# Spreading a background convolution over four units instead of five, with GpSimd's instructions in smaller pieces

## The chip, the cores and the metric

The kernel runs on one core of one Trainium2 chip. The core has five engines with a queue of instructions each, which start in the order in which the program issued them: TensorE (PE in the profile; PEld is its weight load), VectorE (DVE), ScalarE (ACT), GpSimd (POOL) and SyncE (SP), which here issues the DMAs. The metric is the device time of one execution in microseconds, as the median of several runs.

## The reference

A sequence of 2048 tokens with 1024 channels, in 32-bit floats, passes two kinds of layers in turn, A, B, A, B:

```python
def _A_ref(q, k, v, shift_k, ssm_k, ssm_D):
    ...
    kv = k_shift * v
    ...
    y = y + kv * ssm_D[None, None, :]
    return q * y

def _B_ref(x, w1, b1, w2, b2):
    h = jnp.einsum("bsd,df->bsf", x, w1) + b1
    ...
    h = r * r
    out = jnp.einsum("bsf,fd->bsd", h, w2) + b2
    return out

x = A_q
x = x + _A_ref(_layernorm(x, axis=-1), A_k, A_v, A_shift_k, A_ssm_k, A_ssm_D)
x = x + _B_ref(_layernorm(x, axis=-1), B_w1, B_b1, B_w2, B_b2)
x = x + _A_ref(_layernorm(x, axis=-1), A_k, A_v, A_shift_k, A_ssm_k, A_ssm_D)
x = x + _B_ref(_layernorm(x, axis=-1), B_w1, B_b1, B_w2, B_b2)
```

`k_shift` is a causal convolution of length 4 over `k`; `y` is a causal convolution over the whole sequence, channel by channel, of `kv` with `ssm_k`. It depends on neither `x` nor the layer, so it is computed once. In B, `r` is `h` where positive, and F, the width of `h`, is 3584.

## The kernel before

**The main work.** The tokens are cut into four blocks of 512. One unit is layer B of one block in one of the two rounds; ORDER lists the eight units as pairs (round, block): (0,0), (1,0), (0,1), (0,2), (1,1), (0,3), (1,2), (1,3). Units 5 and 6 are worked together. A unit runs in steps of 12 matmuls of 512 columns (each product is made of three, from a high and a low half of both operands, lines 344 to 346). Kind m1 makes `h`, kind m2 the output. A usual unit has 4 chunks of 28 steps, 112 in all; unit 0 has 134, of which the first 8 belong to the start of the kernel, and unit 1 has 124. 16 steps at the start of unit 0, 28 at its end and 24 at the start of unit 1 work on half a block each, and carry half the tokens. The weights of coming steps are loaded by SP into `wr`, cast by ScalarE into the high half of `whl` (line 1103) and subtracted by VectorE into the low half (line 1111); six `whl` buffers stand in a ring. Some pairs of halves are stored and loaded again later. The m1 result passes ScalarE and VectorE (lines 1588 to 1596) and comes back as the operand of m2; `evict` (line 1711) adds m2's result to the output block. `add_b2` (line 1831) adds the output bias to that block near the start of a unit, on GpSimd, 1024 elements at a time.

**The background work.** The long convolution is computed by blocks of 256 tokens in a transformed space. Token block 0 is done at the start of the kernel. For the others (sb = 1, 2, 3) it runs between the steps of the main loop, as Python generators that issue a few instructions each time they are advanced:

- `fwd_x` and `fwd_g` transform `kv` and `ssm_k`, eight column chunks for each sb, and store the results. Both are advanced once by each `fwd_tick`; FWD_RATE says how many ticks a step of a unit gives them. They share two PSUM banks (`pt`) with the inverse transforms through `take`, `hold` and `give`.
- `prod_stream` goes over sb, 16 groups of channels and three types. For each it loads two operands (`cx`, `cg`, two buffers each), and for the two blocks j = 2 sb and 2 sb + 1 `mult` multiplies them on GpSimd (line 534): 128 x (j + 1) elements on each partition, 384 to 1024, into `cp` (three buffers). Two advances later `red` sums over the blocks on VectorE (line 538). After a group's last product come, each one or more advances later, `fold` and `butterfly` on GpSimd (lines 684, 688, 689), a cast on ScalarE and subtractions on VectorE (lines 563, 570), the inverse transform on TensorE (for sb = 2 and 3 two groups in one), a copy and a store to `yd`.

The result for a token block is needed when the next unit prepares its input. When 18 steps of a unit are left, the main loop calls `close_conv` for the next unit's block, which advances the streams until that block is done. Whatever it issues stands in each engine's queue ahead of the following step.

**The pace.** Each step adds `pace[u]` to `owed`, and `prod_stream` is advanced while something is owed, up to 1.06 times the step's rate; an advance that issued a product returns its size in thousands of elements per partition. In the last 19 steps of a unit the rate is a fifth, in half steps a tenth, and `fwd_tick` isn't called in either. Blocks 1 and 2 share one pace over units 0 to 2, block 3 has its own over units 3 and 4. The pace is the work over the steps, in which the last 19 of a unit count a fifth, less a slack (PACE_SLACK); half steps count in full.

After the convolution is done, and from unit 4 on, `make_t` forms sums of the weights for unit 7 in the buffers that the convolution no longer needs.

Of the kernel before, what the change touches and what calls it, by code (L numbers as in the profile page):

```python
# [19 lines left out]
S, D, F = 2048, 1024, 3584  # L20
P = 128
T = 512
NT = T // P
NB = S // T
# [4 lines left out]
BL = 256  # L29
NBL = S // BL  # L30
BT = T // BL
CG = 64
NG = D // CG
CU = 2 * CG
EPS = 1e-5
ORDER = [(0, 0), (1, 0), (0, 1), (0, 2), (1, 1), (0, 3), (1, 2), (1, 3)]
# [9 lines left out]
AHEAD_0 = 4  # L46
BURST = 1.06
FIN = "GGG"
PACE_SLACK = {1: 74, 3: 10}
PACE_TO = {1: 2}  # L50
PLAIN = 1
FILL = (16, 12, 8)
WINO = (7,)
# [20 lines left out]
PIECES = ((0, 0), (0, 1), (1, 0), (1, 1))  # L74
WLO = {"b": "GGGV", "x": "GGGV"}
PREP_PACE = 0.2
FWD_RATE = {0: 1.4, 1: 1.4, 2: 1.4, 3: 1.1, 4: 1.1, 5: 1}


class Later:  # L80
# [168 lines left out]
def tile_h3_mlp(ctx: ExitStack, tc: tile.TileContext, q, kT, vT, shk, ssmT, ssmD, w1, b1, w2, b2,  # L249
                fwd_t, pro_t, inv_t, sgn_t, out):  # L250
    nc = tc.nc
    V, A, G, PE, SY = nc.vector, nc.scalar, nc.gpsimd, nc.tensor, nc.sync
# [268 lines left out]
    def fwd_tick():  # L521
        for g in streams:
            next(g, None)
# [4 lines left out]
    def prod_stream():  # L528
        lag = plag
        sums, inv = [0, 0], [0, 0]  # L530

        def mult(st, xt, gt, j):
            pr = cv.tile([P, CU, j + 1], F32, name="cp", bufs=3)
            G.tensor_mul(pr.rearrange("p c i -> p i c"), xt[:, 0:j + 1], gt[:, j::-1])  # L534
            st["pr"] = pr

        def red(st, sm, ty, jj):
# [109 lines left out]
        for n, (sb, g, ty) in enumerate(units):  # L647
            while n not in when:
                if (sb, g // 2) in fwd_done:
                    load(n)  # L650
                else:
                    lag.tick()
                    yield None
            while lag.n < when[n] + 2:
                lag.tick()
                yield None
            if ty == 0:
                while sums[0] - sums[1] >= 2:
                    lag.tick()
                    yield None  # L660
                sums[0] += 1
                sm = cv.tile([P, 3, BT, CU], F32, name="sm", bufs=2)
                if g % 2 == 0:
                    pair = {}
            for jj in range(BT):
                j = BT * sb + jj
                st = {"pair": pair}
                mult(st, *got[n], j)
                lag.at(2, red, st, sm, ty, jj)
                if jj == BT - 1:  # L670
                    if ty == 2:
                        lag.at(3, fin, st, sm, sb, g, 0)
                    fill(n)
                lag.tick()
                yield (j + 1) * CU * 1e-3
# [5 lines left out]
        return t[:, e].rearrange("p (n c) -> p n c", c=CG)  # L681

    def fold(E, s):
        E.tensor_add(s[:, 1:3], s[:, 1:3], s[:, 0:1].to_broadcast([P, 2, s.shape[2]]))  # L684

    def butterfly(E, s):
        y = s[:, 1:3].rearrange("p r (j u c) -> p u (r j) c", u=2, c=CG)
# [55 lines left out]
    def prep_a(l, b):  # L743
        mv = pre.tile([P, NT, 2], F32, name="mv", bufs=2)
        xs = [load_x(l, b, 0), load_x(l, b, 1)]
        for _ in range(3):
            yield
        for tt in range(NT):
            stats(xs[tt], mv[:, tt])
            if tt + 2 < NT:  # L750
                xs.append(load_x(l, b, tt + 2))
            yield
            yield
            yield
        ve, sd = rstd_a(mv)
        yield
        lnx[l, b] = mv, rstd_b(ve, sd)
        yield
# [120 lines left out]
    def prep_rows(l, b, kept):  # L879
        yield from prep_a(l, b)  # L880
        mv, r = lnx.pop((l, b))
        for tt in range(NT):
            x = load_x(l, b, tt)
            y = pre.tile([P, D], F32, name="px", bufs=2)
            SY.dma_start(y, YD[b][:, tt])
            for _ in range(4):
                yield
            combine(x, y, mv[:, tt, 0:1], r[:, tt:tt + 1])
            yield
            m = pre.tile([P, 1, 2], F32, name="mv2", bufs=4)  # L890
            stats(x, m[:, 0])
            ve, sd = rstd_a(m)
            yield
            SY.dma_start(X1[b][:, tt], x)
            kept.append(scale_bias(m, ve, sd))
            yield
# [8 lines left out]
    NU = len(ORDER)  # L905
# [671 lines left out]
    pds = prod_stream()  # L1577
# [3 lines left out]
    lag = slag  # L1581
# [246 lines left out]

    def add_b2(st, accs):
        for a in accs:  # L1830
            G.tensor_add(a, a, st["t"])

    def store_out(accs, l, b):
        for tt in range(NT):
# [284 lines left out]
    last_step = {}  # L2119
# [3 lines left out]
    p6_at = {s: i for s, (k, u, c, a, i, *_) in enumerate(steps) if k == "ja" and a == 6}  # L2123
    jb_at = min(s for s, (k, *_) in enumerate(steps) if k == "jb")
    start_step = {u: (last_step[u - 1] + 1 if u else 0) for u in range(NU)}
    work = {sb: 3 * NG * CU * 1e-3 * sum(BT * sb + jj + 1 for jj in range(BT)) for sb in range(1, NB)}
    WIN = {sb: min(u for u in range(NU) if ORDER[u][1] == sb) for sb in range(1, NB)}
    pace = {}
    lo_u = 0
    for sb in range(1, NB):  # L2130
        if WIN[sb] > lo_u:
            group = [x for x in range(sb, NB) if PACE_TO.get(x, x) == PACE_TO.get(sb, sb)]
            hi_u = WIN[group[-1]]
            total = sum(work[x] for x in group)
            n = sum(last_step[u] + 1 - start_step[u] - 19 * (1 - PREP_PACE) for u in range(lo_u, hi_u))
            for u in range(lo_u, hi_u):
                pace[u] = total / (n - PACE_SLACK[sb])
            lo_u = hi_u
    owed = town = 0.0
    fowed = 0.0  # L2140
    accs = []
# [4 lines left out]

    def close_conv(nb):
        while nb not in done:
            if next(pds) is None:
                fwd_tick()  # L2150

    for s, (k, u, c, a, i, tts, w) in enumerate(steps):
        if s < 2 * AHEAD_0:
# [2 lines left out]
        if u != cur_u:  # L2156
            cur_u = u
            if u:
                xT = nxt[0] if u == JU + 2 else nxt
            bst = {}  # L2160
            if u == JU:
                jb = ORDER[JU + 1][1]
                lag.at(10, j_places)
                for tt in range(NT):
                    lag.at(4 + tt, j_rows_load, jb, tt)
                    lag.at(7 + tt, j_rows_norm, rn, tt)
                    lag.at(11 + 3 * tt, j_flip, tt)
                    lag.at(12 + 3 * tt, j_xsums, tt, xT, 0)
                    lag.at(13 + 3 * tt, j_xsums, tt, xT, 1)
            elif u in WINO:  # L2170
                wacc, rp = {}, {}
                lag.at(11, load_wacc, wacc, b)
                lag.at(34, load_b2, bst)
                lag.at(38, add_b2w, bst, wacc)
            else:
                if not (u and direct[u - 1]):
                    accs = []
                    lag.at(5, load_acc, accs, b)
                lag.at(12, load_b2, bst)
                lag.at(16, add_b2, bst, accs)  # L2180
# [17 lines left out]
        if k == "m1":  # L2198
# [9 lines left out]
            for kk in range(4):  # L2208
                t = slice(kk * P, (kk + 1) * P)
# [8 lines left out]
        elif k == "ja":  # L2218
# [9 lines left out]
            for kk in range(4):  # L2228
                t = slice(kk * P, (kk + 1) * P)
# [16 lines left out]
        elif k == "jb":  # L2246
# [9 lines left out]
            for tt in range(NT):  # L2256
                t = slice(tt * P, (tt + 1) * P)
# [7 lines left out]
        elif k == "w2":  # L2265
# [7 lines left out]
            for n in range(2):  # L2273
                t = slice(n * P, (n + 1) * P)
# [11 lines left out]
        else:  # L2286
# [5 lines left out]
            for tt in tts:  # L2292
                t = slice(tt * P, (tt + 1) * P)
# [12 lines left out]
            if direct[u] and c == NCH - 1 and a == 0 and i == 0 and tts[0] == 0:  # L2306
                close_conv(ORDER[u + 1][1])
                spare = []
                closed[0] = True
                while len(spare) + 4 < AHEAD[u]:  # L2310
                    got = take(1, True)
                    if got:
                        spare += got
                    else:
                        fwd_tick()
                        plag.tick()
                closed[0] = False
                nxt = (mw.tile([P, KT, T], F32R, name="xh", bufs=1), mw.tile([P, KT, T], F32R, name="xl", bufs=1))
                ready = set()
                half, evict1, stage = chain(accs, b, *nxt, ready)  # L2320
# [6 lines left out]
        if u == JU:  # L2327
            nxt = []if s == start_step[u] else nxt
        elif u + 1 < NU and not direct[u]:
            n = s - start_step[u]  # L2330
            at = J_PREP if u + 1 == JU else 28
            if n == at:
                pa = prep_a(*ORDER[u + 1])
                if u + 1 == JU:
                    rn = []
                    pa = chain_of(prep_rows(*ORDER[JU + 1], rn), pa)
            elif n > at and pa is not None and next(pa, 0) == 0:
                pa = None
            if u in WINO and left == W_PREP:
                nxt = prep_w(*ORDER[u + 1], lag)  # L2340
            elif u not in WINO and left == 18:
                while pa is not None:
                    if next(pa, 0) == 0:
                        pa = None
                close_conv(ORDER[u + 1][1])
                nxt = prep_b(*ORDER[u + 1], lag)
        if u >= WMAKE and len(done) == NB and not tgen:
            tgen.append(make_t())
# [11 lines left out]
        while todo > 0:  # L2360
            x = next(pds, 0)
# [5 lines left out]
            else:  # L2367
                todo -= x
                owed -= x
        fowed += FWD_RATE.get(u, 2) * (0.0 if busy or len(tts) < NT else 1.0)  # L2370
        while fowed >= 1:
# [52 lines left out]
```

## Time and profile before

| | us |
|---|---|
| median of 3 runs | 2677.67 |
| lowest and highest | 2674.93, 2677.69 |
| the profiled execution | 2678.93 |
| its span in the trace | 2677.1 |

The profile is of one execution. Its page gives each engine's busy time and share, the costliest groups of instructions by line, and the DMA issues; the trace behind it is asked for the waits of an engine, for instructions in order of time, and for tables by stretch of the span. A row of a timeline reads: start, duration, engine, line, operation, what it writes from what it reads, count, and in brackets the idle time of the engine just before with what ended it. A row of waits reads: total us, how often, the longest. The clock is the share of its full speed that TensorE was granted. The row of a line gives the shortest, the median and the longest duration in ns.

### The profile page before, as it was taken

What the parts mean: (1) busy time and instruction counts of PE and PEld (TensorE: products, weight loads), DVE (VectorE), ACT (ScalarE), POOL (GpSimd) and SP (SyncE); (2) the same over time, 40 slices, a digit from 0 to 9 for tenths busy, and PEclk for the clock granted to TensorE, in tenths of its full rate; (3) what the DMA queues carried; (4) which work ended last, traced back from release to release, by engine and by line L of the source; (5) the groups of instructions that cost most, each with busy time, mean ns of one, the idle gap of its engine ahead of it and who ended that gap; (6) DMA issues with size and microseconds to landing.
All of it is one profiled execution on the core that took longest, in us unless ns stands there. A gap on an engine that the chain in (4) does not pass through costs nothing.

```text
span 2677.1 us, 36183 instructions
## 1 busy us (share of the span) xinstructions
PE 2621.7 (98%) x12400; PEld 2195.7 (82%) x12400; DVE 1987.5 (74%) x2993; ACT 1116.0 (42%) x1947; POOL 851.7 (32%) x532
## 2 busy tenths in 40 slices
PE   7999999999999999999999999999999999999999
PEld 7888787888888888888888888887787888788887
DVE  7879888789887877779777777655788674745565
ACT  4454344434444333343333422345655443345443
POOL 2336665355642645427554275100000030001000
PEclk9999999999999999999999999999999999999999
DMA  8789898689989898888987888777899988746556
GB/s 259 260 301 313 294 307 282 240 294 374 339 296 317 315 337 299 267 306 307 337 298 257 308 301 315 266 243 285 304 308 303 367 296 310 265 164 197 174 171 206
DMA packets 390680, 761.59 MB, mean 284 GB/s; under 512 B 45392, under 2 KB 160736, under 8 KB 390496
## 3 DMA queue, kind: packets, MB, share of 16 engines
q1 hardware_dynamic: 390496, 759.28, 82.4%
q8 instruction: 98, 1.61, 0.2%
q14 instruction: 86, 0.70, 0.1%
HBM read 581.92 MB, written 177.21 MB: 284 GB/s over the span
## 4 chain that ended last, share of the span: by engine, by line
PE 76%; DVE 9%; DMA 8%; issue 2%; SPq 2%; ACT 2%; POOL 1%; DVEq 0%; ACTq 0%; POOLq 0%
PE p L344 22%; PE p L345 22%; PE p L346 22%; DMA wr<-w 3%; PE p L1189 2%; PE pt L345 2%; PE pt L344 2%; PE pt L346 2%; DVE whl L1111 1%; DMA whl<-wd_m 1%; DMA cx<-xd 1%; DMA cg<-gd 0%; DVE st L705 0%; SPq L1955 0%; PE pt L429 0%
## 5 line engine op out<-in xcount | busy, mean ns | idle before, releaser
L534 POOL TENSOR_TENSOR cp<-cx,cg 128x384 f32<-128x384 f32 (+5 forms) x288 | 546.1, 1909 | 572.0 <-DVE sm L538 367.0
L344 PE MATMUL p<-xh,whl 128*128 128x512 f32 (+1 forms) x1504 | 576.8, 384 | 4.8 <-ACT fx L1907 2.9
L346 PE MATMUL p<-xh,whl 128*128 128x512 f32 (+1 forms) x1504 | 572.4, 381 | 0.8 <-POOL whl L1111 0.8
L345 PE MATMUL p<-xl,whl 128*128 128x512 f32 (+1 forms) x1504 | 572.4, 381 | 0.1
L1111 DVE TENSOR_TENSOR whl<-wr,whl 128x512 fp32r<-128x512 f32 x535 | 452.2, 858 | 95.6 <-ACT whl L1103 82.6
L1103 ACT CAST whl<-wr 128x512 fp32r<-128x512 f32 x550 | 334.7, 618 | 383.0 <-PE p L346 243.8
L344 PE MATMUL p<-whl,rh 128*128 128x512 f32 x1204 | 475.5, 395 | 3.8 <-ACT whl L1103 2.8
L345 PE MATMUL p<-whl,rh 128*128 128x512 f32 x1204 | 470.7, 391 | 1.3 <-POOL whl L1111 0.8
L346 PE MATMUL p<-whl,rl 128*128 128x512 f32 x1204 | 470.4, 391 | 0.0
L344 PEld LDWEIGHTS p<-xh,whl 128*128 128x128 f32 x1504 | 283.5, 189 | 59.5 <-ACT fx L1907 4.6
L346 PEld LDWEIGHTS p<-xh,whl 128*128 128x128 f32 x1504 | 283.1, 188 | 55.3 <-POOL whl L1111 1.0
L345 PEld LDWEIGHTS p<-xl,whl 128*128 128x128 f32 x1504 | 283.3, 188 | 52.3 <-DVE xl L1502 0.3
L344 PEld LDWEIGHTS p<-whl,rh 128*128 128x128 f32 x1204 | 227.3, 189 | 50.8 <-ACT whl L1103 3.8
L345 PEld LDWEIGHTS p<-whl,rh 128*128 128x128 f32 x1204 | 227.3, 189 | 48.1 <-DVE whl L1111 1.6
L346 PEld LDWEIGHTS p<-whl,rl 128*128 128x128 f32 x1204 | 226.9, 188 | 47.7
L1596 DVE TENSOR_TENSOR rl<-wr,rh 128x512 fp32r<-128x512 f32 x140 | 140.2, 1002 | 165.5 <-ACT rh L1591 165.5
L538 DVE TENSOR_REDUCE sm<-cp 128x128 f32<-128x384 f32 (+5 forms) x288 | 249.8, 874 | 11.4 <-POOL cp L534 11.4
L1588 ACT ACTIVATE wr<-p,b1t 128x512 f32<-128x512 f32 x138 | 95.2, 690 | 356.5 <-PE p L346 355.5
L2036 POOL TENSOR_TENSOR acc<-acc,px 128x512 f32<-128x512 f32 x8 | 11.7, 1481 | 454.0 <-DMA wr<-td 451.0
L1711 DVE TENSOR_TENSOR acc<-p,acc 128x512 f32<-128x512 f32 x152 | 99.8, 686 | 74.5 <-PE p L346 74.5
L684 POOL TENSOR_TENSOR sm<-sm 128x512 f32<-128x512 f32 x48 | 69.1, 1440 | 130.6 <-DVE sm L538 117.8
L1688 POOL TENSOR_TENSOR acc<-acc,px 128x512 f32<-128x512 f32 x6 | 7.7, 1318 | 267.6 <-DMA px<-b 267.6
(431 smaller groups left out, 4233.8 us busy)
## 6 DMA issues: line engine op xcount, KB each, us to landing
whl<-wd_m SPq DMA_DIRECT2D x334, 512.0 KB, 5.5
wr<-w SPq DMA_DIRECT2D x440, 256.0 KB, 5.4
wd_m<-whl SPq DMA_DIRECT2D x70, 512.0 KB, 6.2
wr<-td SPq DMA_DIRECT2D x104, 256.0 KB, 4.5
cx<-xd SPq DMA_DIRECT2D x48, 512.0 KB, 6.2
cg<-gd SPq DMA_DIRECT2D x48, 512.0 KB, 7.1
rh<-rd SPq DMA_DIRECT2D x84, 256.0 KB, 5.8
gd<-fg SPq DMA_DIRECT2D x72, 256.0 KB, 6.2
```

What stands on the lines that cost most here:

```text
L344: PE.matmul(o, lh, rh, start=start, stop=False, skip_group_check=skip)
L345: PE.matmul(o, lh, rl, start=False, stop=False, skip_group_check=skip)
L346: PE.matmul(o, ll, rh, start=False, stop=stop, skip_group_check=skip)
L534: G.tensor_mul(pr.rearrange("p c i -> p i c"), xt[:, 0:j + 1], gt[:, j::-1])
L538: V.tensor_reduce(sm[:, ty, jj], st["pr"], axis=AX.X, op=OP.add)
L684: E.tensor_add(s[:, 1:3], s[:, 1:3], s[:, 0:1].to_broadcast([P, 2, s.shape[2]]))
L1103: A.copy(t[:, 0], raws[n]["t"])
L1111: ENG[e[n % len(e)]].tensor_sub(t[:, 1], raws[n]["t"], t[:, 0].bitcast(F32))
L1189: PE.matmul(o, lh, r, start=start, stop=stop)
L1588: A.activation(r, st["o"], AF.Relu, bias=b1t[:, st["f"]:st["f"] + 1])
L1596: V.tensor_sub(st["lo"], st["r"]["t"], st["hi"].bitcast(F32))
L1711: V.tensor_add(accs[tt][:, d], o, accs[tt][:, d])
```

## The change

Constants: one slack of 30, a weight PACE for each of units 0 to 3, at most G_BLOCKS = 3 blocks of 128 elements in one GpSimd product, and new rates for the forward streams.

```diff
-PACE_SLACK = {1: 74, 3: 10}
-PACE_TO = {1: 2}
+PACE_SLACK = 30
+PACE = (0.82, 0.98, 1.08, 1.12)
+G_BLOCKS = 3
...
-FWD_RATE = {0: 1.4, 1: 1.4, 2: 1.4, 3: 1.1, 4: 1.1, 5: 1}
+FWD_RATE = {0: 1.4, 1: 1.6, 2: 1.7, 3: 1.7}
```

The product of one j is issued as several instructions over parts of the j + 1 blocks: 3 blocks stay one, 4 become 2 + 2, 5 become 2 + 3, 6 become 3 + 3, 7 become 2 + 2 + 3 and 8 become 2 + 3 + 3. `fold` becomes two instructions of 256 elements instead of one of 512, and `add_b2` four of 256 instead of one of 1024.

```diff
-            G.tensor_mul(pr.rearrange("p c i -> p i c"), xt[:, 0:j + 1], gt[:, j::-1])
+            n = -(-(j + 1) // G_BLOCKS)
+            cuts = [(j + 1) * k // n for k in range(n + 1)]
+            for a, e in zip(cuts, cuts[1:]):
+                G.tensor_mul(pr[:, :, a:e].rearrange("p c i -> p i c"), xt[:, a:e],
+                             gt[:, j - a:j - e if e <= j else None:-1])
...
-        E.tensor_add(s[:, 1:3], s[:, 1:3], s[:, 0:1].to_broadcast([P, 2, s.shape[2]]))
+        for k in (1, 2):
+            E.tensor_add(s[:, k], s[:, k], s[:, 0])
...
-            G.tensor_add(a, a, st["t"])
+            for d in range(0, D, BL):
+                G.tensor_add(a[:, d:d + BL], a[:, d:d + BL], st["t"][:, d:d + BL])
```

The pace: the work of all three blocks is spread over units 0 to 3, each weighted by PACE.

```diff
-    pace = {}
-    lo_u = 0
...
-                pace[u] = total / (n - PACE_SLACK[sb])
-            lo_u = hi_u
+    work = sum(3 * NG * CU * 1e-3 * (j + 1) for j in range(BT, NBL))
+    span = {u: (last_step[u] + 1 - start_step[u] - 19 * (1 - PREP_PACE)) * PACE[u] for u in range(len(PACE))}
+    pace = {u: work * PACE[u] / (sum(span.values()) - PACE_SLACK) for u in span}
```

Near the end of unit 3 `close_conv` is called for the last block, and it advances the main loop's own list of later work where the stream has ended.

```diff
         while nb not in done:
-            if next(pds) is None:
+            x = next(pds, 0)
+            if x is None:
                 fwd_tick()
+            elif x == 0:
+                lag.tick()
...
-                close_conv(ORDER[u + 1][1])
+                close_conv(ORDER[u + 1][1] if u < 3 else NB - 1)
```

More of the change, by code (lines that the diff above doesn't have):

```diff
@@ L2125, in tile_h3_mlp @@
     start_step = {u: (last_step[u - 1] + 1 if u else 0) for u in range(NU)}
-    work = {sb: 3 * NG * CU * 1e-3 * sum(BT * sb + jj + 1 for jj in range(BT)) for sb in range(1, NB)}
-    WIN = {sb: min(u for u in range(NU) if ORDER[u][1] == sb) for sb in range(1, NB)}
-    pace = {}
-    lo_u = 0
[L2130 to L2136, printed above, removed]
-                pace[u] = total / (n - PACE_SLACK[sb])
-            lo_u = hi_u
+    work = sum(3 * NG * CU * 1e-3 * (j + 1) for j in range(BT, NBL))
+    span = {u: (last_step[u] + 1 - start_step[u] - 19 * (1 - PREP_PACE)) * PACE[u] for u in range(len(PACE))}
+    pace = {u: work * PACE[u] / (sum(span.values()) - PACE_SLACK) for u in span}
     owed = town = 0.0
```

## The prediction

> **What bounds the kernel now.** I read the page's first part, then a table of busy time by stretch of the span, one stretch per unit of the main loop (the bounds are my reading of where the bias rows are added, some 40 us into each unit).
>
> ```profile
> span 2677.1 us, 36183 instructions
> PE 2621.7 (98%) x12400; PEld 2195.7 (82%) x12400; DVE 1987.5 (74%) x2993; ACT 1116.0 (42%) x1947; POOL 851.7 (32%) x532
> ...
> 135.00:505.00 370.00, 354.62 (x1678) 297.58 (x1678) 308.23 (x452) 161.72 (x290) 195.84 (x152) 0.98 0.89 296
> 505.00:845.00 340.00, 336.93 (x1744) 288.44 (x1743) 287.13 (x416) 148.44 (x264) 156.81 (x94) 1.00 0.89 311
> 845.00:1175.00 330.00, 329.46 (x1565) 276.66 (x1564) 264.44 (x367) 123.50 (x220) 151.51 (x87) 1.00 0.89 306
> 1175.00:1505.00 330.00, 329.65 (x1550) 276.07 (x1549) 255.63 (x329) 117.90 (x207) 164.41 (x82) 1.00 0.86 301
> 1505.00:1800.00 295.00, 293.48 (x1322) 243.71 (x1321) 196.91 (x285) 90.69 (x159) 103.59 (x53) 1.00 0.80 286
> ```
>
> The columns are the stretch, its length, then PE, PEld, DVE, ACT and POOL (busy, count), granted clock, DMA share, GB/s. TensorE (PE) is the bound: in units 1 to 4 (rows two to five) it idles 3.1, 0.5, 0.4 and 1.5 us. The change adds no matmul and removes none, so it can only win idle time of PE, and there is little outside unit 0, which idles 15.4 us. The waits of PE from 135 to 520 us, and the stretches of 45 us in which the clock was not full:
>
> ```profile
> PE pt L429 <- DVE fx L376: 8.7, 4, 6.3
> PE p L344 <- ACT whl L1103: 2.8, 1, 2.8
> PE pt L604 <- DVE fg L493: 2.5, 1, 2.5
> ...
> 270.00:315.00 45.00, 38.74 (x171) 32.29 (x170) 38.20 (x55) 12.55 (x23) 30.46 (x26) 0.92 1.00 331
> 405.00:450.00 45.00, 42.53 (x204) 35.78 (x203) 40.79 (x57) 19.77 (x36) 28.21 (x21) 0.96 0.82 262
> 450.00:495.00 45.00, 40.80 (x174) 32.39 (x173) 34.52 (x67) 19.68 (x34) 10.12 (x8) 0.97 0.90 306
> ```
>
> A stall of PE costs twice: 6.3 us of idle is followed by a mean clock of 0.92 over 45 us (another 0.08 x 45 = 3.6 us), 2.5 us by 0.96 (1.8 us), 2.8 us by 0.97 (1.3 us). The first and third waits are for VectorE behind background work of the convolution; the second belongs to the chain at the end of unit 0, which the change doesn't touch.
>
> **The pacing, walked by hand.** One thousand elements of product count 1; the three late blocks hold 3 x 16 x 0.128 x (3+4+5+6+7+8) = 202.75. Before, 110.6 (blocks 1 and 2) over units 0 to 2 gives 0.4417 a step, and 92.2 over units 3 and 4 gives 0.502. Walking the loop with these rates (half steps at a tenth, the last 19 steps of a unit at a fifth) gives 91, 57, 56, 51 and 33 multiplies in units 0 to 4. The multiplies of the trace (POOL column, line 534) by the same stretches:
>
> ```profile
> 135.00:505.00 370.00, 124.45 (x92) 0.98 0.89 296
> 505.00:845.00 340.00, 110.10 (x58) 1.00 0.89 311
> 845.00:1175.00 330.00, 111.86 (x56) 1.00 0.89 306
> 1175.00:1505.00 330.00, 124.49 (x51) 1.00 0.86 301
> 1505.00:1800.00 295.00, 75.23 (x31) 1.00 0.80 286
> ```
>
> 92, 58, 56, 51, 31: the walk holds. Now the new rule. Weighted spans: (134-15.2) x 0.82 = 97.4, (124-15.2) x 0.98 = 106.6, (112-15.2) x 1.08 = 104.5 and x 1.12 = 108.4, together 417.0; less the slack of 30, 387.0. So 202.75/387.0 = 0.5239, times PACE: 0.4296, 0.5134, 0.5658, 0.5868. What is issued: unit 0, 90 full steps, 17 half, 19 half and slow, 39.6; unit 1, 81 full, 24 half, 19 slow, 44.8; unit 2, 93 full, 19 slow, 54.8; unit 3 up to its closing step (18 steps left), 93 full, 54.6. The sum is 193.8, so **9.0 are not issued when close_conv for the last block is called**: five multiplies of 1024 and four of 896. The half steps are the reason: the spans count them as full ones. close_conv issues all that is left within one step, down to the last inverse transform, and TensorE's queue holds that inverse ahead of the next step's matmuls. Before, no closing call found anything to do.
>
> **The price of that burst.** Single pieces, and the tail of the conv before:
>
> ```profile
> L534 POOL TENSOR_TENSOR cp<-cx,cg x288: 1002/1866/2878, 188.7 to 1680.4; 128x384 f32<-128x384 f32 x48, 128x640 f32<-128x640 f32 x48, 128x896 f32<-128x896 f32 x48
> L688 POOL TENSOR_TENSOR sm<-sm x49: 727/1062/1197, 106.5 to 1692.2; 128x256 f32<-128x256 f32 x49
> ...
> 1680.44 2.42 POOL L534 TENSOR_TENSOR cp<-cx,cg 128x1024 f32<-128x1024 f32 x1 [1.62 <-DVE sm L538]
> 1689.48 1.21 DVE L538 TENSOR_REDUCE sm<-cp 128x128 f32<-128x1024 f32 x1
> 1693.31 0.41 ACT L563 CAST yh<-sm 128x256 fp32r<-128x256 f32 x1 [1.53 <-POOL sm L688]
> 1696.34 0.76 DVE L570 TENSOR_TENSOR yl<-sm,yh 128x256 fp32r<-128x256 f32 x2
> 1695.02 0.28 PE L344 MATMUL pt<-yh,ih 128*128 128x256 f32 x1
> 1696.81 0.39 PE L345 MATMUL pt<-yl,ih 128*128 128x256 f32 x1 [1.52 <-DVE yl L570]
> ...
> 2170.23 0.39 PE L344 MATMUL p<-whl,xl 128*128 128x512 f32 x1
> 2172.95 0.39 PE L344 MATMUL p<-whl,xl 128*128 128x512 f32 x1
> ```
>
> Undisturbed, 384 elements take 1.00 us and 256 take 0.73 (the least of each), so 1024 in pieces is 0.73 + 2 x 1.00 = 2.73 and 896 is 2 x 0.73 + 1.00 = 2.46. Nine multiplies: 5 x 2.73 + 4 x 2.46 = 23.5 us on GpSimd. The fold and butterfly of group 14 stand between them in its queue: 4 x 0.73 = 2.9. After the last product comes a chain: reduce 1.21, fold and butterfly of group 15 2.9, cast 0.41, the two subtractions 0.76: 5.3. Together 31.7 us. Against it stands GpSimd's lead: by the walk the last multiply of before (1680.44) is issued in one step and the inverse three steps later (1695.02); a step is 12 matmuls, 2.72 us from 2170.23 to 2172.95; so GpSimd was 14.6 - 8.2 = 6.4 us ahead. The stall is 31.7 - 6.4 = **25.3 us**. Its bounds: with a lead of four steps (10.9 us) 20.8; upward, the last three pairs of operands are loaded within the burst, two buffers deep:
>
> ```profile
> cx<-xd SPq DMA_DIRECT2D x48, 512.0 KB, 6.2
> cg<-gd SPq DMA_DIRECT2D x48, 512.0 KB, 7.1
> ```
>
> 7.1 us of landing against the 5.2 us of one unit's two multiplies leaves up to 1.9 a load, three loads, 5.7: 31.0. These loads stand in SP's queue ahead of the next weights, and VectorE's reduces ahead of the next splits; both wait for GpSimd, and the next step's matmuls for both, but no longer than for the inverse. The clock afterwards: +3.6, as after the 6.3 us.
>
> **The other parts.** Unit 0: j = 2 stays one piece, j = 3 becomes two, each fold two, each bias row four. What this does where PE lost 6.3 us:
>
> ```profile
> 286.45 2.48 DVE L1711 TENSOR_TENSOR acc<-p,acc 128x512 f32<-128x512 f32 x4
> 290.27 1.30 POOL L684 TENSOR_TENSOR sm<-sm 128x512 f32<-128x512 f32 x1 [3.72 <-DVE sm L538]
> 290.70 3.69 DVE L374 SCALAR_TENSOR_TENSOR fx<-fx,shkt 128x512 f32<-128x512 f32 x3
> 293.80 3.99 POOL L534 TENSOR_TENSOR cp<-cx,cg 128x384 f32<-128x384 f32 x3
> ...
> L374 DVE SCALAR_TENSOR_TENSOR fx<-fx,shkt x72: 706/752/2799, 146.0 to 1403.7; 128x512 f32<-128x512 f32 x72
> L1111 DVE TENSOR_TENSOR whl<-wr,whl x535: 644/686/2905, 143.4 to 2665.1; 128x512 fp32r<-128x512 f32 x179
> ```
>
> VectorE works without a gap there; its three operations of 0.75 take 3.69 instead of 2.25 while GpSimd runs, but the multiplies there are 384 already, so the pieces save under 1 us. What moves more is the pace: 0.012 less a step is one multiply later after 40 steps, which may undo the clash or make another. The two stalls that can move cost 8.7 + 2.5 + 3.6 + 1.8 = 16.6; I take a third, -5 (from -16 to +6, a new stall of the smaller kind with its clock). Units 1 to 3 get 66 multiplies each for 57, 56, 51; VectorE's share there was 84, 80 and 77%, 9 to 15 reduces of about 1 us more are some 12 us of 330, and blocked time falls (below): 0, from -3 (their idle) to +8. The 1.5 us at 1696.81 goes: -1.5. Pieces add 336 + 48 + 60 instructions on GpSimd; from 0.73 and 1.00 the fixed part of one is 0.18, so 80 us more on an engine idle two thirds of the time: 0 outside the burst. make_t starts at the first step of unit 4, as VectorE is free there: 0.
>
> Sum: profiled execution 2678.9 us (span 2677.1 and 1.8 around it) + 25.3 + 3.6 - 5 - 1.5 = 2701.3; the median of the runs is 1.3 below that execution, so **2700 us**.
>
> **Rivals.** (a) Faster: the relief of VectorE decides, and the closing call finds next to nothing. Mechanism: VectorE's operations with two operands wait for GpSimd's running instruction (L1111 686 at the median, 2905 at most); shorter pieces halve that, the two stalls of unit 0 go with their clock, and so does the 1.5: 2677.7 - 16.6 - 1.5 = 2660. It decides where fewer than three multiplies (6.4 us of lead) are left at closing. For it: VectorE is 83% busy in unit 0. Against it: the walk reproduces the trace within 2 multiplies, and nine are left. [...] (b) Worse: the burst, and the denser units 2 and 3 let GpSimd fall behind (its busy share there was 46 and 50%, with the pieces and 28 and 17% more products some 65%), so that each of the 14 paired inverses ahead of the burst waits as at 1696.81: 2700 + 14 x 1.5 = 2721. Against it: PE idled under 1 us in those units. (c) Nothing to tell: the burst is there, but all of the 16.6 and a lead of six steps, 16.3 us, pay for it: 2677.7 + 15.4 + 3.6 - 16.6 - 1.5 = 2679.
>
> **How the numbers follow.** Forecast 0.70, (a) 0.14, (b) 0.10, (c) 0.06. The forecast's own range, 20.8 to 31.0 and unit 0 from -11 to +4, is 2688 to 2714; to leave no more than 2 in 10 outside I go to 2670 and 2720. A measurement tells 0.2% (5.4 us). Faster: most of (a), 0.14; same: (c) and the forecast's low edge, 0.09; slower: 0.77.
>
> **What would show it.** One stretch near 1470 us where PE idles over 20 us at an inverse's matmul that waits for yl (line 570), GpSimd running nine multiplies without pause before it, then half a clock for some us; no multiply after it; line 534 with about 89, 66, 67, 66 products in units 0 to 3. Wrong if that stall is under 10 us, if multiplies go on into the last 18 steps of unit 3, or if units 1 to 3 idle more than 10 us elsewhere.

## The result, and the profile after

The changed kernel takes 2746.62 us (median of 4 runs, 2743.26 to 2747.59) against 2677.68 us (4 runs, 2674.93 to 2682.81): a ratio of 1.0253, 95% interval 1.0235 to 1.0271, or 69 us more. That is outside the predicted range, on the forecast's side of it. The page of the profile after, its heads and the three groups that matter most here:

```profile
span 2741.4 us, 36606 instructions
PE 2636.0 (96%) x12400; PEld 2206.3 (80%) x12400; DVE 1894.8 (69%) x2995; ACT 1114.2 (41%) x1947; POOL 957.1 (35%) x976
...
L538 POOL TENSOR_TENSOR cp<-cx,cg 128x384 f32<-128x384 f32 (+1 forms) x624 | 628.7, 1040 | 374.3 <-DMA cg<-gd 172.4
L1117 DVE TENSOR_TENSOR whl<-wr,whl 128x512 fp32r<-128x512 f32 x535 | 426.6, 810 | 102.1 <-ACT whl L1109 95.8
...
L1838 POOL TENSOR_TENSOR acc<-acc,px 128x256 f32<-128x256 f32 x80 | 68.4, 891 | 99.0 <-DMA px<-b 99.0
```

The diff shifts the lines: the product is L538 now, its reduce L543, the subtractions after the inverse's cast L575, the weights' cast and split L1109 and L1117, the bias L1838, the matmul triple L345 to L347. The number of matmuls is the same, so two subtractions say where the 64.3 us of longer span went: TensorE's busy time rose by 14.3 us (2636.0 - 2621.7; the same matmuls, some at a lower clock: its mean is 0.986 for 0.996) and its idle time by 50.0 us (105.4 for 55.4). VectorE, on the other hand, is busy 92.7 us less: the shorter GpSimd instructions did free it, as rival (a) said (1885.3 us in e2, the pieces alone, and 1990.8 in e3, without pieces, for 1987.5 before), and TensorE gains little by it (e3 and e4 below).

Where the idle time lies shows in the table by unit. A unit begins here where VectorE starts its first subtraction at L1596 (L1602 after); columns as in the prediction's table. Before:

```profile
142.00:530.00 388.00, 372.46 (x1826) 315.05 (x1825) 324.82 (x492) 170.06 (x305) 197.87 (x154) 0.98 0.87 288
530.00:858.00 328.00, 325.09 (x1594) 274.75 (x1593) 283.08 (x393) 141.10 (x252) 156.18 (x92) 1.00 0.92 321
858.00:1188.00 330.00, 329.46 (x1571) 276.89 (x1570) 257.96 (x357) 122.26 (x218) 151.65 (x88) 1.00 0.88 303
1188.00:1518.00 330.00, 329.65 (x1545) 275.84 (x1544) 254.50 (x328) 118.54 (x210) 163.08 (x81) 1.00 0.86 299
1518.00:1855.00 337.00, 334.57 (x1513) 277.54 (x1512) 222.53 (x342) 116.20 (x202) 100.79 (x52) 1.00 0.82 292
```

After:

```profile
142.00:531.00 389.00, 373.29 (x1834) 316.31 (x1833) 310.96 (x491) 170.38 (x306) 211.96 (x222) 0.98 0.87 287
531.00:872.00 341.00, 330.06 (x1606) 278.37 (x1606) 275.46 (x412) 143.17 (x256) 204.68 (x198) 0.98 0.93 319
872.00:1229.00 357.00, 346.68 (x1641) 290.18 (x1640) 287.49 (x403) 132.10 (x240) 222.87 (x229) 0.99 0.90 317
1229.00:1591.00 362.00, 328.92 (x1512) 274.49 (x1511) 231.10 (x313) 112.50 (x202) 221.58 (x248) 0.96 0.79 276
1591.00:1919.00 328.00, 328.00 (x1465) 271.84 (x1465) 159.26 (x328) 111.34 (x186) 13.52 (x16) 1.00 0.80 274
```

Unit 0 is as long as before. Units 1, 2 and 3 are 13, 27 and 32 us longer, unit 4 is 9 us shorter; the sum, 64 us with unit 0, is the whole loss. TensorE idles 10.9, 10.3 and 33.1 us in units 1 to 3, where it idled 2.9, 0.5 and 0.4. Part of unit 2's growth is moved work, which unit 4 gives back: 70 more matmuls there, 48 fewer in unit 4. A fuller DMA does not show: its share (last column but one) in units 1 to 3 is 0.93, 0.90 and 0.79, for 0.92, 0.88 and 0.86. TensorE's largest waits after, window by window (units 0, 1, 2 and 3), tell what was late:

```profile
PE p L345 <- ACT whl L1109: 8.5, 2, 6.1
PE pt L430 <- DVE fx L377: 5.0, 1, 5.0
...
PE p L347 <- POOL whl L1117: 4.4, 1, 4.4
PE pt L345 <- DVE fy L413: 4.3, 1, 4.3
...
PE p L345 <- DMA whl<-wd_m: 8.5, 3, 4.7
...
PE pt L345 <- ACT yh L568: 20.4, 1, 20.4
PE pt L346 <- DVE fx L391: 11.4, 1, 11.4
```

**The forecast burst is there.** GpSimd around the closing call, then TensorE, both after (start, duration, engine, line):

```profile
1493.37 3.16 POOL L538 TENSOR_TENSOR cp<-cx,cg 128x256 f32<-128x256 f32 x3
1498.28 2.44 POOL L538 TENSOR_TENSOR cp<-cx,cg 128x256 f32<-128x256 f32 x3 [1.75 <-DVE sm L543]
1502.33 8.00 POOL L538 TENSOR_TENSOR cp<-cx,cg 128x256 f32<-128x256 f32 x9 [1.61 <-DVE sm L543]
...
1511.66 2.37 POOL L538 TENSOR_TENSOR cp<-cx,cg 128x256 f32<-128x256 f32 x3
...
1515.46 7.95 POOL L538 TENSOR_TENSOR cp<-cx,cg 128x256 f32<-128x256 f32 x9
...
1506.12 0.28 PE L347 MATMUL pt<-yh,fl 128*128 128x256 f32 x1
1526.76 0.58 PE L345 MATMUL pt<-yh,ih 128*128 128x256 f32 x1 [20.37 <-ACT yh L568]
```

The last 27 pieces, nine multiplies, run from 1493.37 to 1523.41, and the inverse that TensorE holds in its queue comes at 1526.76: 33.4 us of chain for the 31.7 predicted. The multiplies were not without a pause: two waits of 1.75 and 1.61 us for VectorE's sums stand among them. GpSimd's lead over TensorE was 13 us (1506.40 - 1493.37) instead of 6.4, so the stall is 20.4. The clock in it and right behind it, by stretch:

```profile
1506.00:1527.00 21.00, 0.63 (x5) 0.43 (x3) 10.22 (x11) 1.81 (x4) 20.11 (x26) 0.60 0.35 112
1527.00:1531.00 4.00, 3.93 (x16) 3.46 (x17) 0.78 (x2) 1.24 (x3) 0.07 (x1) 0.55 0.01 2
```

The clock is low in both, but 1506 to 1527 is the stall itself, in which there is next to nothing to slow (0.63 us of work). Of work only 4 us ran at 0.55 (from 1531 on the rows have 1.00): 1.8 us lost. A shorter stall cost more: after the 4.4 us of waiting at 545 us (below) TensorE worked 5.2 us at 0.51, some 2.6 us lost. An expectation below that counts the clock after the 20.4 us as ten microseconds misreads it; the 3.4 us of clock that others count for a short stall are half of a stretch like that from 544.15 to 550.98 us, 6.8 us at 0.50, in which TensorE worked 5.1.

**What the forecast did not have** begins at 530 us. GpSimd there, after:

```profile
530.26 14.31 POOL L1838 TENSOR_TENSOR acc<-acc,px 128x256 f32<-128x256 f32 x16
544.53 1.26 POOL L1117 TENSOR_TENSOR whl<-wr,whl 128x512 fp32r<-128x512 f32 x1
```

Up to here some weight splits are GpSimd's (15 in all, the last at 548.5 us). This one stands behind the bias rows, which are one run of 16 pieces now: 14.31 us, where the four whole rows took 10.85 us (row of before below). The matmul that reads the split waits 4.4 us. At 1261 us the same run meets the denser products:

```profile
1261.42 13.36 POOL L1838 TENSOR_TENSOR acc<-acc,px 128x256 f32<-128x256 f32 x16
1274.74 10.81 POOL L538 TENSOR_TENSOR cp<-cx,cg 128x256 f32<-128x256 f32 x12
...
1277.42 1.22 DVE L543 TENSOR_REDUCE sm<-cp 128x128 f32<-128x1024 f32 x1 [9.43 <-POOL cp L538]
1278.56 4.92 DVE L575 TENSOR_TENSOR yl<-sm,yh 128x256 fp32r<-128x256 f32 x2
1283.40 0.68 DVE L391 TENSOR_TENSOR fx<-pt,fx 128x512 fp32r<-128x512 f32 x1
...
1264.10 0.38 SPq L1099 DMA_DIRECT2D wr<-w  x1
1277.41 0.32 SPq L639 DMA_DIRECT2D cx<-xd  x1
...
1278.30 0.86 SPq L1105 DMA_DIRECT2D whl<-wd_m  x2
...
1284.13 0.58 PE L346 MATMUL pt<-fx,fh 128*128 128x256 f32 x1 [11.45 <-DVE fx L391]
```

The product behind the run of bias rows is late; VectorE has its reduce next in its queue and does nothing for 9.43 us, with the forward transform's subtraction (L391) behind it; SP holds the next operand load until a product frees the buffer, from 1264.5 to 1277.4, with the weights' loads behind it; and TensorE waits 11.45 us for L391. GpSimd works without a gap from 1261.42 to 1285.55 us, though it is busy only 61% of this unit; behind it VectorE, SP and TensorE wait in turn. The lateness comes from the order in the queues here, not from an engine's work in total.

### The profile page after: what moved, and what is told of

The parts are those of the page before. It is cut to its first block, busy times and chain, and to the rows that moved or that the text cites. A ratio compares the mean times of both kernels' runs of the same rounds, so it can differ in the third digit from the quotient of the medians.

```text
span 2741.4 us, 36606 instructions
## 1 busy us (share of the span) xinstructions
PE 2636.0 (96%) x12400; PEld 2206.3 (80%) x12400; DVE 1894.8 (69%) x2995; ACT 1114.2 (41%) x1947; POOL 957.1 (35%) x976
## 3 DMA queue, kind: packets, MB, share of 16 engines
q8 instruction: 98, 1.61, 0.2%
## 4 chain that ended last, share of the span: by engine, by line
PE 72%; DVE 10%; DMA 9%; POOL 4%; issue 2%; ACT 2%; SPq 2%; DVEq 0%; POOLq 0%; ACTq 0%
PE p L345 21%; PE p L346 21%; PE p L347 21%; DMA wr<-w 3%; POOL cp L538 2%; DMA cg<-gd 2%; PE p L1195 2%; PE pt L346 2%; PE pt L347 2%; PE pt L345 2%; DVE whl L1117 1%; POOL acc L1838 1%; DMA yt<-yd 1%; DMA whl<-wd_m 1%; DVE sm L543 1%
## 5 line engine op out<-in xcount | busy, mean ns | idle before, releaser
L538 POOL TENSOR_TENSOR cp<-cx,cg 128x384 f32<-128x384 f32 (+1 forms) x624 | 628.7, 1040 | 374.3 <-DMA cg<-gd 172.4
L345 PE MATMUL p<-xh,whl 128*128 128x512 f32 (+1 forms) x1504 | 579.1, 385 | 9.1 <-DMA whl<-wd_m 4.9
L347 PE MATMUL p<-xh,whl 128*128 128x512 f32 (+1 forms) x1504 | 574.3, 382 | 4.4 <-POOL whl L1117 4.4
L1117 DVE TENSOR_TENSOR whl<-wr,whl 128x512 fp32r<-128x512 f32 x535 | 426.6, 810 | 102.1 <-ACT whl L1109 95.8
L345 PE MATMUL p<-whl,rh 128*128 128x512 f32 x1204 | 477.3, 396 | 12.1 <-ACT whl L1109 8.5
L1109 ACT CAST whl<-wr 128x512 fp32r<-128x512 f32 x550 | 334.1, 618 | 375.1 <-PE p L347 245.2
L347 PE MATMUL p<-whl,rl 128*128 128x512 f32 x1204 | 472.2, 392 | 0.0
L345 PEld LDWEIGHTS p<-xh,whl 128*128 128x128 f32 x1504 | 284.9, 189 | 64.7 <-ACT fx L1914 5.3
L347 PEld LDWEIGHTS p<-xh,whl 128*128 128x128 f32 x1504 | 284.6, 189 | 59.4 <-POOL whl L1117 4.6
L543 DVE TENSOR_REDUCE sm<-cp 128x128 f32<-128x384 f32 (+5 forms) x288 | 249.0, 874 | 52.3 <-POOL cp L538 52.3
L345 PEld LDWEIGHTS p<-whl,rh 128*128 128x128 f32 x1204 | 228.6, 190 | 59.3 <-ACT whl L1109 9.3
L347 PEld LDWEIGHTS p<-whl,rl 128*128 128x128 f32 x1204 | 228.0, 189 | 48.1
L1602 DVE TENSOR_TENSOR rl<-wr,rh 128x512 fp32r<-128x512 f32 x140 | 123.1, 879 | 192.9 <-ACT rh L1597 192.8
L2043 POOL TENSOR_TENSOR acc<-acc,px 128x512 f32<-128x512 f32 x8 | 12.7, 1614 | 582.0 <-DMA wr<-td 580.7
L690 POOL TENSOR_TENSOR sm<-sm 128x256 f32<-128x256 f32 x96 | 81.7, 860 | 69.3 <-DVE sm L543 69.1
L1838 POOL TENSOR_TENSOR acc<-acc,px 128x256 f32<-128x256 f32 x80 | 68.4, 891 | 99.0 <-DMA px<-b 99.0
```

The source lines that it names most:

```text
L345: PE.matmul(o, lh, rh, start=start, stop=False, skip_group_check=skip)
L347: PE.matmul(o, ll, rh, start=False, stop=stop, skip_group_check=skip)
L538: G.tensor_mul(pr[:, :, a:e].rearrange("p c i -> p i c"), xt[:, a:e], gt[:, j - a:j - e if e <= j else None:-1])
L543: V.tensor_reduce(sm[:, ty, jj], st["pr"], axis=AX.X, op=OP.add)
L690: E.tensor_add(s[:, k], s[:, k], s[:, 0])
L1109: A.copy(t[:, 0], raws[n]["t"])
```

## The experiments

Times are medians; each ratio is against runs of the kernel before on the same chip (medians 2679.75, 2680.41 and 2678.34 us for the first four, the next four and the last three). Idle is the profiled execution's span less TensorE's busy time; that time of before is 2621.7 us. Where two kernels were run beside different runs of before, a second figure takes each over its own.

| kernel | us | ratio, 95% interval | PE busy | PE idle |
|---|---|---|---|---|
| before | 2677.68 | | 2621.7 | 55.4 |
| after | 2746.62 | 1.0253, 1.0235 to 1.0271 | 2636.0 | 105.4 |
| e1_no_closing | 2722.98 | 1.0161, 1.0146 to 1.0176 | 2636.1 | 86.6 |
| e2_pieces_only | 2686.23 | 1.0020, 1.0011 to 1.0029 | 2626.9 | 57.6 |
| e3_pace_only | 2756.28 | 1.0285, 1.0270 to 1.0300 | 2639.5 | 115.8 |
| e4_bias_whole | 2736.86 | 1.0217, 1.0200 to 1.0234 | 2634.8 | 98.6 |
| e5_forward_slow | 2719.31 | 1.0138, 1.0111 to 1.0164 | 2638.0 | 84.2 |
| e6_forward_fast | 2691.58 | 1.0038, 1.0023 to 1.0053 | 2628.4 | 61.1 |
| e7_bias_spread | 2707.88 | 1.0101, 1.0083 to 1.0119 | 2633.2 | 68.9 |
| e8_best_try | 2683.17 | 1.0005, 0.9995 to 1.0015 | 2623.9 | 58.9 |
| e9_loads_later | 2716.40 | 1.0135, 1.0120 to 1.0150 | 2633.6 | 79.2 |
| e10_slack_50 | 2723.45 | 1.0165, 1.0150 to 1.0180 | 2635.4 | 86.8 |
| e11_transform_wait | 2704.40 | 1.0086, 1.0070 to 1.0103 | 2629.6 | 73.3 |

**The closing call alone (e1).** The kernel after, without the closing call for the last block; what is left over runs on in unit 4.

```diff
+    pace[4] = pace[3]
...
-                close_conv(ORDER[u + 1][1] if u < 3 else NB - 1)
+                close_conv(ORDER[u + 1][1])
```

> The changed kernel, but the last block is closed where it was before, at the end of unit 4, and unit 4 goes on at unit 3's pace; nothing else differs. Theory 'closing burst': the 20.4 us wait near 1526 us and its 20.5 us at half clock go, so 2746.6 - 20.4 - 10.3 = about 2716 us, and the other new waits (467, 545, 640, 930, 942 and 1284 us) stay. Rival 'only moved': the nine multiplies cost the same wherever they run, 2740 us or more.

2722.98 us, between the two expectations and nearer the first: the burst costs 23.6 us (2746.62 - 2722.98), or 25.7 with each over its own runs of before. In the profiles TensorE's idle time falls by 18.8 us and its busy time not at all, so the clock after the long stall is no term to speak of. 43 us over the kernel before are left, and they are not the burst.

**The pieces alone (e2).** The kernel before with the products, folds and bias rows in pieces, at the old pace.

```diff
+G_BLOCKS = 3
...
-            G.tensor_mul(pr.rearrange("p c i -> p i c"), xt[:, 0:j + 1], gt[:, j::-1])
+            n = -(-(j + 1) // G_BLOCKS)
...
-            G.tensor_add(a, a, st["t"])
+            for d in range(0, D, BL):
+                G.tensor_add(a[:, d:d + BL], a[:, d:d + BL], st["t"][:, d:d + BL])
```

> The kernel before with the pieces alone (products of at most 384 elements, folds and bias rows in 256); pace and closing as before. Theory 'pieces cost': 16 bias pieces take 14.3 us where 4 rows took 10.9, the split of a weight behind them on GpSimd is late as at 545 us in the changed kernel (4.6 us and 3.4 us of clock more), so 2684 to 2690 us. Rival 'pieces relieve': VectorE's blocked time falls by 95 us as in the changed kernel, waits of unit 0 shrink, 2665 to 2675 us.

2686.23 us, 6.5 more than before (interval 2.9 to 7.8), as the first expectation has it: 444 more instructions on an engine that idles two thirds of the time are not quite free. The run of bias rows at the start of unit 1, in the kernel before:

```profile
529.62 10.85 POOL L1831 TENSOR_TENSOR acc<-acc,px 128x1024 f32<-128x1024 f32 x4
```

and in e2, with TensorE's largest wait in unit 1 behind it (the same wait is 0.8 us before):

```profile
526.48 14.31 POOL L1838 TENSOR_TENSOR acc<-acc,px 128x256 f32<-128x256 f32 x16
...
PE p L347 <- POOL whl L1117: 3.5, 1, 3.5
```

**The pace alone (e3), and the bias rows whole (e4).** Both start from the kernel after. In e3 all three kinds of pieces are taken back; e4 takes back the last line only.

```diff
-            for d in range(0, D, BL):
-                G.tensor_add(a[:, d:d + BL], a[:, d:d + BL], st["t"][:, d:d + BL])
+            G.tensor_add(a, a, st["t"])
```

> The changed kernel with the products, the folds and the bias rows whole again; pace, forward rates and closing as changed. Theory 'pace and closing': the burst stays (nine whole multiplies and the chain, about 18 us and 10 us of clock), and the waits behind the bias rows stay but are some 3 us shorter each, so 2725 to 2740 us. Rival 'pieces': the loss comes mostly from the pieces, 2705 us or less.

> The changed kernel with only the bias rows whole again (4 instructions of 1024 per unit for 16 of 256). Theory 'bias pieces': the wait at 545 us goes with its clock (8 us), those at 930, 942 and 1284 us shrink by 3 us each, about 2728 us. Rival 'pace': those waits come from the products queued behind, and only the 8 us go or less, 2738 us or more.

e3 takes 2756.28 us, above both of its expectations and 10 more than the kernel after (8 with each over its own runs of before): at the new pace the pieces together win time, at the old one they lose 6.5. e4 takes 2736.86, 10 less than after (12), close to its rival's 2738: cutting the bias rows alone is a loss, and by e3 less e4 cutting the products and folds is worth 19 us where GpSimd is crowded. The pieces are not what costs; what does must be sought in the pace, the rates and the burst.

**The forward rates (e5, e6).** e5 is e1 with the old rates, e6 is e2 with the new ones (and 1.7 in unit 4).

```diff
-FWD_RATE = {0: 1.4, 1: 1.6, 2: 1.7, 3: 1.7}
+FWD_RATE = {0: 1.4, 1: 1.4, 2: 1.4, 3: 1.1, 4: 1.1, 5: 1}
```

> The first experiment's kernel (closing as before) with the forward streams at the rates of the kernel before (1.4, 1.4, 1.4, 1.1, 1.1). Products per unit stay 89, 66, 67, 59, 7. Theory 'forward rate': the waits at 640 and 1284 us, which are for operands of forward transforms, go with their clock, 8 and 17 us of 2723, so 2698 to 2705 us. Rival 'products': those waits come from GpSimd's queue behind the bias rows and merely change their place, 2715 us or more.

> The kernel before with the pieces (as in the second experiment, 2686 us) and in addition the faster forward streams (1.6 in unit 1, 1.7 in units 2 to 4); products at the old pace. Theory 'forward rate': 2700 us or more. Rival 'products': 2684 to 2692 us.

e5 takes 2719.31, 3.7 less than e1, which is within the spread of its own runs (2713.69 to 2725.31); e6 takes 2691.58, 5.4 more than e2. Both lie where the rival 'products' had them, and the rates are a small term from either side. That leaves the pace of the products, with all that follows them: from e2 to e5, with the same pieces, the same rates and no burst, 33.1 us (32.4). So the loss of 69 us divides, one step at a time and each kernel over its own runs of before, into pieces 6.5, pace 32, rates 4, burst 26. In another order the terms differ, as e3 shows for the pieces.

**The bias rows apart from each other (e7).** e1 with one row every second step instead of four at once, so that products and splits can pass between them.

```diff
-    def add_b2(st, accs):
-        for a in accs:
+    def add_b2(st, accs, tt):
+        for a in accs[tt:tt + 1]:
...
-                lag.at(12, load_b2, bst)
-                lag.at(16, add_b2, bst, accs)
+                lag.at(10, load_b2, bst)
+                for tt in range(NT):
+                    lag.at(13 + 2 * tt, add_b2, bst, accs, tt)
```

> The first experiment's kernel with the bias rows issued one row (four pieces) every second step instead of all 16 pieces in one step; the instructions are the same. Theory 'run of bias rows': GpSimd is never more than 3.4 us behind for their sake, the waits at 546, 932, 944 and 1285 us (23.4 us and some 13 us of clock) go, about 2690 us. Rival 'density': VectorE and the DMA queue are full at this pace with or without the run, 2712 us or more.

2707.88 us, 15 less than e1, without a change to the pace or to the number of GpSimd's instructions; that is 18 us above the 2690 expected and 4 under the rival's 2712. TensorE's largest wait in unit 2:

```profile
PE p L345 <- DMA whl<-wd_m: 5.7, 3, 5.1
```

Of the waits of the kernel after, which e1 has too, that for GpSimd's split (4.4 us) is gone from unit 1, and of the 11.4 us for L391 2.3 are left. What remains over the kernel before is, in the profiles, 13.5 us of idle and 11.5 us of slower matmuls. The wait shown is for a load of weights. SP's wait for a product that must free the operand's buffer, in the same unit, first in the kernel before, then in e1 and in e7:

```profile
SPq L634 <- POOL cp L534: 6.5, 4, 2.8
```

```profile
SPq L639 <- POOL cp L538: 41.2, 14, 15.1
```

```profile
SPq L639 <- POOL cp L538: 38.5, 18, 6.3
```

From e1 to e7 the sum of these waits hardly changes, and the longest falls from 15.1 to 6.3 us. So the sum is no measure of what TensorE loses; the long single waits went with the run of bias rows.

**The operand loads later (e9).** e7, with the next operands asked for at the following group's first product and not right after the last one of this group.

```diff
-                    fill(n)
+                elif n:
+                    fill(n - 1)
```

> The kernel with the bias rows spread (2708 us), and in it the loads of operands of the unit after next issued one product later, so that they stand less long in SP's queue waiting for GpSimd to free their buffer. Theory 'weights behind operand loads': SP's wait for products in unit 2 (38 us) falls below 20 us, the wait for a weight load at 932 us (5.2 us and 3.4 us of clock) goes, 2695 to 2701 us. Rival 'density elsewhere': GpSimd waits for its operands instead, 2706 us or more.

SP's wait in unit 2 falls from 38.5 to 24.0 us:

```profile
SPq L639 <- POOL cp L538: 24.0, 9, 6.4
```

and TensorE's waits for weights in that unit are gone, so that chain is real. But the kernel takes 2716.40 us, 8.5 more than e7 (10.6): unit 0 is 9 us longer than there, with TensorE's waits at 23.8 us in place of 16.4, the new ones mostly for VectorE's splits and ScalarE's results. The time is the rival's (2706 or more) without its reason: GpSimd's wait for operand loads in unit 2 is 37.5 us, for 33.8 in e7. The place of the loads isn't a way out; it moves the waiting.

**The burst dissolved by more density (e10).** After, with a slack that leaves nothing to the closing call.

```diff
-PACE_SLACK = 30
+PACE_SLACK = 50
```

> The changed kernel with a slack of 50 for 30. By the walk the pace rises by 5% (0.453, 0.541, 0.597, 0.619), the last product is issued five steps ahead of the closing call, and that call finds nothing. Theory 'closing burst': the wait of 20 us and its 10 us of clock go, the waits behind the bias rows grow a little, 2715 to 2730 us. Rival: the 5% more pace costs as much as the burst, 2740 us or more.

2723.45 us, as expected: the burst is gone by this way too, for the same 23 us as in e1. TensorE's idle time, 86.8 us, is that of e1 (86.6), but it is elsewhere. The largest wait of e10 over units 0 to 4, which stands at 8.5 us in three waits after:

```profile
PE p L345 <- DMA whl<-wd_m: 15.0, 7, 5.1
```

**Two tries for a faster kernel (e8, e11).** e8 is the kernel before with products and folds in pieces and the bias rows whole, but one every second step. e11 is the kernel before in which the forward transform of block 1 waits longer between its parts, meant for the 6.3 us stall of unit 0.

```diff
-        for _ in range(4 if sb == 1 else 7):
+        for _ in range(7):
```

> The kernel before at its own pace, with products and folds in pieces, and the bias rows whole but issued one every second step. By 'run of bias rows' the wait at 542 us (3.7 us and 3.4 us of clock with pieces) goes, and what the pieces win elsewhere remains: 2670 to 2677 us. By 'pieces cost': 2683 us or more.

> The kernel before, in which fwd_x lets seven advances pass between VectorE's product and TensorE's transposes for the first of the late blocks too, where it lets four pass. Theory 'VectorE is late in unit 0': the waits of TensorE for that product (8.7 us in unit 0 and 3.4 us of clock) go, 2664 to 2672 us. Rival: the stall goes to the next instruction that waits for VectorE, 2676 us or more.

e8 takes 2683.17 us, a ratio of 1.0005 with 1 inside the interval: the pieces cost nothing there that the runs could tell, and win nothing. Its median is the bound that 'pieces cost' gave, 3 us under e2.

e11 takes 2704.40, 26 more than its runs of before, though only a wait in unit 0 was changed. In that unit the stall went to the next instruction that waits for VectorE, as the rival said: TensorE waits 9.0 us for weight splits, 6.1 the longest, where it had waited 8.7 and 6.3 for the transform. The products, by units:

```profile
142.00:527.00 385.00, 111.64 (x84) 0.98 0.84 284
527.00:864.00 337.00, 116.22 (x67) 1.00 0.90 314
864.00:1208.00 344.00, 107.99 (x55) 0.99 0.87 304
```

A slower transform postponed the products that need it: unit 0 issues 84 of them instead of 93 and is 3 us shorter, unit 1 has 67 instead of 59. Unit 1 is 9 us longer, where the change with nearly the same number of products makes it 13 us longer, and TensorE idles 9.4 us in it for 2.9 before. But unit 2 has 55 products as before and is 14 us longer, with 25 more matmuls and 4.4 us of idle for 0.5. So products per unit are not the whole reason; other postponed work goes along with them, and which part of it costs was not tried. No kernel tried was faster than the one before.

## Why the prediction was wrong

**What failed** is the sentence "Units 1 to 3 get 66 multiplies each ...: 0, from -3 (their idle) to +8". The kernel without the burst (e1) is 43 us over the kernel before; 32 of it are the denser products with what follows them, 4 the rates, 6.5 the pieces. The step took busy shares (VectorE 77 to 84%, GpSimd at two thirds) and concluded that more work of this kind fits. Shares say what an engine could carry; the waits that were followed came from the order in which single instructions stand in line. GpSimd runs bias rows, products and, up to unit 1, weight splits in one queue; VectorE has reduces ahead of splits and forward transforms, SP operand loads ahead of weight loads. As long as products came thinly, GpSimd was nearly always ahead of those who wait for it: in unit 2 SP's longest wait for its buffers was 2.8 us, and 15.1 in e1. At 66 products a unit, that lead is too short for a run of bias rows of 13 to 14 us. Spreading this run (e7) gave back 15 us; that much of the mechanism is shown. The prediction had the queues in hand, since it used them for the burst, and did not ask the same of the run of bias rows at each unit's start.

**"Pieces add 336 + 48 + 60 instructions ...: 0 outside the burst"**: 6.5 us at the old pace, in part by way of the same run (10.85 us became 14.31; with that run whole and spread, e8, 3 us of it are gone); at the new pace the pieces win 8 to 10 us (e3). Neither is 0, and the second shows that a price taken at the old density doesn't hold at the new one.

**The burst**: right in its number of multiplies, in its mechanism and in the inverse that waits, though that waits for the cast `yh` (L568) and not for `yl`; sized at 25.3 + 3.6, it costs 23.6 to 25.7. That the size came out so near is in part luck: the lead was 13 us, twice the one taken, and above even the four steps of the lower bound, and the chain took 1.7 us longer than priced. The clock costs 1.8 us: what counted was the work that ran before it was full again, 4 us at 0.55, and not the length of the stall, 20.4 us. The 3.6 came from a mean over 45 us in which the stall itself lay. Shorter stalls were followed by a low clock too: in the kernel before, 6.3 us of idle that end at 299.08 by 0.50 up to 304.61 us, and 2.5 us of idle that end at 444.11 by 0.75 from 446 to 450 us.

**The pacing walk**: right. Units 0 to 3 issue 136, 134, 167 and 188 pieces of product (L538's counts between the bounds of units above), which are about 91, 68, 67 and 63 multiplies for 89, 66, 67 and 66, and unit 4 none.

**Unit 0, -5 (from -16 to +6)**: 0, inside its bounds; the wait of 6.3 us became one of 5.0, that for the weights' cast grew from 2.8 to 8.5. **The 1.5 us at 1696.81** went with the tail of the convolution, as said.

**The rivals**: (a)'s relief of VectorE is there, 92.7 us of it, and not on the path. (b) had the right cause, GpSimd falling behind, at the wrong place: the inverses' waits for `yl` sum to 1.3 us over the four units, and the stalls came at the bias rows, the forward transform and the weight loads. The prediction's own sign of error, more than 10 us of idle elsewhere in units 1 to 3, is what happened: 54.3 us less the 20.4 leaves 33.9, for 3.8 before.

**Still open**: e7's remaining 27 us are shown as waits and slower matmuls, but not tried one by one; some of them move when touched (e9, e10), so a sum over single causes may not exist. Which of the queues starts those delays is not shown either: the runs do not separate GpSimd's queue from VectorE's and SP's, and in e11 a unit is longer at an unchanged number of products.

## What to carry to other kernels

Price a denser background stream by the queues it shares: for each engine and for the loads, list what stands behind the instruction that will wait, and compare the longest run on the producing engine with its lead, not its busy share with 100%. Look for unrelated runs on the same engine (here four bias rows at once) before thickening the stream, and space those first. A stall put off by finishing work earlier can be bought with as much idle time where that work goes (e10).

## What the runs showed of the hardware

One VectorE operation with two operands lasted ten times its shortest time, over several GpSimd instructions in a row and not over one. After, in unit 2; the first row gives the shortest, median and longest of the 24 operations of this line in ns:

```profile
L417 DVE TENSOR_TENSOR fx<-fy x24: 672/856/6943, 171.5 to 1329.8; 128x512 f32<-128x512 f32 x24
...
923.33 6.94 DVE L417 TENSOR_TENSOR fx<-fy 128x512 f32<-128x512 f32 x1
...
920.43 5.63 POOL L538 TENSOR_TENSOR cp<-cx,cg 128x384 f32<-128x384 f32 x6
926.01 1.40 POOL L690 TENSOR_TENSOR sm<-sm 128x256 f32<-128x256 f32 x2
927.37 1.68 POOL L538 TENSOR_TENSOR cp<-cx,cg 128x256 f32<-128x256 f32 x2
929.00 0.73 POOL L694 TENSOR_TENSOR sm<-sm 128x256 f32<-128x256 f32 x1
```

It lasted over the ends of some eight GpSimd instructions that followed one another without a gap; GpSimd's next instruction started several times in a row while this operation had not ended. That is a reading of their times, not an experiment, and why this one operation took so long no run shows. The kernel before has the splits on VectorE (L1111) at 647 to 2905 ns from 142 to 1855 us, where GpSimd is busy 769.6 us, and at 681 to 694 ns from 2350 us to the end, where it is busy 10.2 us; VectorE's statistics of one operand (L705) stay at 668 to 695 ns from 142 to 1855 us. The 6.94 us are the exception: over the whole kernel the splits at L1117 average 810 ns for 858 before (801 in e2, the pieces alone, and 870 in e3, without pieces), so with smaller pieces they were shorter on the whole.
